# One 8 KB row per partition instead of two of 4 KB in the K and V loads of a decode kernel

## The chip, the cores and the metric

The kernel runs on one core of one Trainium2 chip. The metric is the time on the device in microseconds (us); below it is the median of several executions. A profile is a separate execution, recorded by the hardware profiler, and its span is a few us shorter than the timed runs.

## What is computed

Two identical layers of a decoder for one new token of each of B = 4 sequences. A layer is attention over a cache and then a gated FFN, each with a layernorm ahead and a residual add behind:

```python
def _A_ref(x, k_cache, v_cache, wq, wo):          # Hq = 32 heads, 8 K/V heads, Sk = 8192, Dh = 128
    q = (x @ wq).reshape(B, Sq, Hq, Dh) ...
    k = jnp.repeat(k_cache, rep, axis=1)           # rep = 4
    v = jnp.repeat(v_cache, rep, axis=1)
    scores = jnp.einsum("bhqd,bhkd->bhqk", q, k) * (Dh ** -0.5)
    p = _softmax(scores, axis=-1)
    o = jnp.einsum("bhqk,bhkd->bhqd", p, v)
    return o...reshape(B, Sq, Hq * Dh) @ wo
def _B_ref(x, w_gate, w_up, w_down):
    return (_silu(x @ w_gate) * (x @ w_up)) @ w_down

x = x + _A_ref(_layernorm(x), A_k_cache, A_v_cache, A_wq, A_wo)
x = x + _B_ref(_layernorm(x), B_w_gate, B_w_up, B_w_down)
# and both lines once more, with the same weights and caches
```

All is bfloat16. Each cache is 4 x 8 x 8192 x 128, 64 MB. Both layers read the same caches and weights. Softmax and the weighted sum over the cache don't depend on the order in which its rows are taken, as long as K and V take them in the same order.

## The kernel before

**Units.** The cache of one batch entry b and one K/V head g is cut into NCH = 4 chunks of CR = 2048 rows (512 KB). A unit is one such chunk, `("k", l, b, g, c)` or `("v", l, b, g, c)`, with l the layer. Two units make a pair, and a pair is what one DMA loads: 1 MB into one buffer, of which each unit uses one half. `KU` (line 251) pairs K units: heads g and g + 1 at the same chunk c. `VU` (line 254) pairs V units: chunks c and c + 1 of the same head.

**Buffers.** `ring` has NRING = 4 buffers of 1 MB, used in turn by K and V; `kept` has 5, in which five V pairs of every batch entry stay from layer 1 to layer 2. A buffer is given back (`release`, line 390) when the second unit of its pair has been issued to TensorE; `pump` (line 372) then issues the next load in the list on the SP queue, which waits for the semaphores of those that still read the buffer.

**A K unit** (`k_front`, line 409, and `k_back`, line 427). Rows of the cache lie on the partitions, 16 to a partition. TensorE transposes the 16 blocks of 128 x 128 into PSUM (line 417), in two halves of 8, each into one of three PSUM banks in turn; each half is copied to one of four `ktp` buffers by DVE or ACT (lines 246 and 248, five of eight to DVE). `k_back` multiplies them with the padded queries (line 433): four matmuls that accumulate all heads of one chunk in one score bank, bank 3 for even c and 4 for odd (`SBANK[c % 2]`). With the last head of a chunk comes `softmax_block` (line 443): a maximum on DVE (line 445) and an exponential with its sum on ACT (line 447). `k_back` of a unit is issued after `k_front` of the next one. After the last unit of the last chunk both are flushed, and `finalize` (line 452) starts the exchange of the maxima and the scaling and transposition of the probabilities, spread over the next units (`run_delayed`).

**A V unit** (`v_unit`, line 508): 32 matmuls with V blocks as weights and 4 probability columns (line 516), accumulated over the chunks of a head.

**Order.** The order of the pairs is written out by hand (lines 296 to 318), in phases: A1 (K of batch 0, layer 1), B1 (K of batch 1 mixed with V of batch 0), then for every b: C1 (V units around the FFN and the next query projection), A2 (K of layer 2 for b, mixed with V), B2 (V of layer 2, mixed with K of layer 1 for b + 2). `mix` (line 263) spreads the shorter list evenly over the longer; it sees pairs only, and there are 16 K pairs to a layer and batch entry. `A_of` (line 275) joins `KU(l, b, c)` for c = 0 to 3. Weight loads are put in at fixed places among the first 32 loads. [...]

Of the kernel before, what the change touches and what calls it, by code (L numbers as in the profile page):

```python
# [102 lines left out]
def bass_interleave_layers__gqa_block_cached__swiglu_ffn__decode_kernel(  # L103
# [13 lines left out]
    _, G, S, Dh = A_k_cache.shape  # L117
# [4 lines left out]
    P = 128  # L122
# [4 lines left out]
    CR = 2048  # L127
# [11 lines left out]
    with ExitStack() as es:  # L139
# [67 lines left out]
        T = _Sync(engines, prog)  # L207
# [41 lines left out]


        def KU(l, b, c):
            return [(("k", l, b, g, c), ("k", l, b, g + 1, c)) for g in range(0, G, 2)]

        def VU(l, b, g):
            return [(("v", l, b, g, c), ("v", l, b, g, c + 1)) for c in range(0, NCH, 2)]
# [7 lines left out]
        def mix(a, b):  # L263
# [9 lines left out]
            return r + b[k:]  # L273

        A_of = lambda l, b, cs: sum((KU(l, b, c) for c in cs), [])
        B_of = lambda l, b, gs: sum((VU(l, b, g) for g in gs), [])
        TAIL1 = [5, 5, 5]
# [60 lines left out]
        for pr in order:  # L338
            kind, l, b, g, c = pr[0]
            if kind == "v" and (g, c) in kept_ix:  # L340
                s = kept_ix[(g, c)]
                buf, key, sm = kept[:, s, :], f"kept{s}", sem_kept[s]
                fresh = l == 0
            else:
                s = nring % NRING
                nring += 1
                buf, key, sm = ring[:, s, :], f"ring{s}", sem_ring[s]
# [24 lines left out]
        def pump():  # L372
            while lptr[0] < len(loads):
                kind, x, sm = loads[lptr[0]]
                if kind == "w":
                    T.dma("sp", x[0], x[1], sm, writes=[x[2]])
                else:
                    pr, buf, key = x
                    if not released.get(key, True):
                        return  # L380
                    released[key] = False
                    kind, l, b, g, c = pr[0]
                    if kind == "k":
                        src = A_k_cache[b, g:g + 2, c * CR:(c + 1) * CR, :].rearrange("i (p t) d -> p i (t d)", p=P)
                    else:
                        src = A_v_cache[b, g, c * CR:(c + 2) * CR, :].rearrange("(i p t) d -> p i (t d)", i=2, p=P)
                    T.dma("sp", buf.rearrange("p (i x) -> p i x", i=2), src, sm, writes=[key])
                lptr[0] += 1

        def release(u):  # L390
# [269 lines left out]
        T.dma("sp", xrow[:], A_x.rearrange("b s d -> (b s) d"), sem_x, writes=["xrow"])  # L660
        T.dma("sp", wq_sb[:], A_wq.rearrange("(kt p) n -> p kt n", p=P), sem("sem_wq"), writes=["wq"])
        pump()
        xb = bank_bf(MISC)
        for nq in range(NQ):
# [10 lines left out]
        def do(u):  # L675
            if u[0] == "k":
                hv = k_front(u)
                if not hold["on"]:
                    flush()
                pending.append((u, hv))  # L680
                if u[3] == G - 1 and u[4] == NCH - 1:
                    flush()
            else:
                v_unit(u)
            run_delayed()
            pump()
# [118 lines left out]
```

## Time and profile before

| | |
|---|---|
| time, median of 3 (range) | 724.67 us (724.6 to 726.92) |
| span of the profile | 718.7 us |
| PE busy | 595.8 us (83%) |
| PE weight loads | 486.6 us (68%) |
| DVE busy | 299.5 us (42%) |
| ACT busy | 235.4 us (33%) |
| read from HBM | 261.36 MB, 364 GB/s over the span |
| K loads | 128 of 1 MB, median 8.0 us from issue to landing |
| V loads into the ring / kept | 88 / 20 of 1 MB, 8.3 / 13.0 us |
| transposes of K (line 417) | 4096, 303.4 us busy |
| score matmuls (line 433) | 1024, 113.8 us busy |
| V matmuls (line 516) | 4096, 128.1 us busy |

Busy time of TensorE overstates its load, since matmuls overlap. A load's time to landing includes the time that it stands behind earlier loads in the queue. "PE" is a matmul, "PEld" the load of its weights, "SPq" the queue that issues the DMAs. A line such as "PE ps L417 <- DMA ring<-in_A_k_cache_dram" says that TensorE's instructions of line 417 stood still for a K load to land; its numbers are the us in total, the times, and the longest.

### The profile page before, as it was taken

To read this page: it belongs to the slowest core of one execution; us is meant where nothing else is said; L and a number is where in the kernel's file an instruction comes from. 1 tells how busy PE (TensorE), PEld (TensorE's weight loads), DVE (VectorE), ACT (ScalarE), POOL (GpSimd) and SP (SyncE) were. 2 spreads that over 40 slices of the span, in tenths; PEclk is the share of its full clock that TensorE was granted. 3 is DMA by queue.
4 is the path that set the end of the run, shared out by engine and by line. 5 is a ranking of instruction groups with operands and counts; after the bars stand their busy time and mean duration, and the time that the engine had idled before them with its cause. 6 is when DMAs were issued, how large, how long until landed. Compare 5 with 4: busy or idle time off the path is not lost.

```text
span 718.7 us, 25091 instructions
## 1 busy us (share of the span) xinstructions
PE 595.8 (83%) x11552; PEld 486.6 (68%) x11552; DVE 299.5 (42%) x635; ACT 235.4 (33%) x296; POOL 0.7 (0%) x6
## 2 busy tenths in 40 slices
PE   3877878887989898897889989987898866999776
PEld 3755656667867676777766776766876666866565
DVE  2544533432445444442355525552255501355401
ACT  0444433320345334430344424530154400255200
POOL 0000000000000000000000000000000000000000
PEclk9999888975699788975799979995599855699755
DMA  8999999999699999999899999999899989599992
GB/s 350 388 388 407 397 399 375 403 401 386 235 374 398 363 353 399 352 411 393 294 391 399 384 403 382 385 409 402 314 386 383 393 339 408 181 370 389 370 402 80
DMA packets 71914, 262.99 MB, mean 366 GB/s; under 512 B 3960, under 2 KB 9856, under 8 KB 71296
## 3 DMA queue, kind: packets, MB, share of 16 engines
q1 hardware_dynamic: 71808, 261.38, 94.9%
q8 instruction: 90, 1.47, 0.8%
q14 instruction: 16, 0.13, 0.0%
HBM read 261.36 MB, written 0.00 MB: 364 GB/s over the span
## 4 chain that ended last, share of the span: by engine, by line
PE 46%; DMA 45%; DVE 3%; issue 3%; SPq 1%; ACT 1%; ACTq 0%
DMA ring<-in_A_k_cache_dram 29%; PE ps L417 24%; DMA ring<-in_A_v_cache_dram 14%; PE ps L516 6%; PE ps L433 6%; PE ps L581 2%; DMA wq_sb<-in_A_wq_dram 2%; PE ps L605 2%; SPq L92 1%; PE ps L557 1%; PE ps L641 1%; PE ps L540 1%; PE ps L488 1%; DVE negm L445 1%; ACT ktp L248 1%
## 5 line engine op out<-in xcount | busy, mean ns | idle before, releaser
L417 PE MATMUL ps<-ident,ring 128*128 128x128 bf16 x4096 | 303.4, 233 | 42.3 <-DMA ring<-in_A_k_cache_dram 42.0
L417 PEld LDWEIGHTS ps<-ident,ring 128*128 128x128 bf16 x4096 | 258.9, 105 | 94.7 <-DMA ring<-in_A_k_cache_dram 52.7
L246 DVE COPY ktp<-ps 128x1024 bf16<-128x1024 bf16 x320 | 215.7, 689 | 205.3 <-PE ps L417 204.0
L248 ACT ACTIVATE ktp<-ps 128x1024 bf16<-128x1024 bf16 x192 | 195.9, 1023 | 267.4 <-PE ps L417 267.4
L433 PE MATMUL ps<-ktp,qpad 128*32 128x512 bf16 x1024 | 113.8, 414 | 3.5 <-ACT ktp L248 3.0
L516 PE MATMUL ps<-pp,ring 128*128 128x4 bf16 x2816 | 88.6, 166 | 27.1 <-DMA ring<-in_A_v_cache_dram 13.5
L516 PEld LDWEIGHTS ps<-pp,ring 128*128 128x128 bf16 x2816 | 82.9, 101 | 37.6 <-issue 19.3
L433 PEld LDWEIGHTS ps<-ktp,qpad 128*32 128x32 bf16 x1024 | 27.6, 93 | 37.9 <-ACT ktp L248 6.4
L573 ACT ACTIVATE lnv<-var,eps_sb 128x4 f32<-128x4 f32 x10 | 3.0, 298 | 145.6 <-DVE var L560 145.6
L524 DVE TENSOR_TENSOR oT<-ps,invL 128x4 bf16<-128x4 f32 x64 | 10.7, 167 | 93.7 <-PE ps L516 93.3
L516 PE MATMUL ps<-pp,kept 128*128 128x4 bf16 x1280 | 39.5, 166 | 8.9 <-DMA kept<-in_A_v_cache_dram 6.2
L516 PEld LDWEIGHTS ps<-pp,kept 128*128 128x128 bf16 x1280 | 37.6, 103 | 11.7 <-issue 6.1
L447 ACT ACTIVATE pp<-ps,negm 128x512 bf16<-128x512 f32 x32 | 22.0, 687 | 31.2 <-DVE negm L445 29.7
L581 PE MATMUL ps<-xnT,wq_sb 128*128 128x4 bf16 x640 | 18.7, 166 | 10.9 <-DMA wq_sb<-in_A_wq_dram 7.8
L445 DVE TENSOR_REDUCE negm<-ps 128x1 f32<-128x512 f32 x32 | 22.1, 690 | 11.7 <-PE ps L433 10.3
L581 PEld LDWEIGHTS ps<-xnT,wq_sb 128*128 128x128 bf16 x640 | 18.1, 104 | 11.4 <-DMA wq_sb<-in_A_wq_dram 7.9
L540 PE MATMUL ps<-oT,wo_sb 128*128 128x4 bf16 x640 | 21.9, 166 | 3.6 <-DVE oT L524 2.6
L540 PEld LDWEIGHTS ps<-oT,wo_sb 128*128 128x128 bf16 x640 | 19.4, 102 | 7.1 <-issue 3.6
L488 PE MATMUL ps<-ident,pp 128*128 128x128 bf16 x128 | 15.0, 311 | 1.0 <-DVE pp L478 1.0
L488 PEld LDWEIGHTS ps<-ident,pp 128*128 128x128 bf16 x128 | 13.0, 145 | 1.1 <-DVE pp L478 1.1
L248 ACT ACTIVATE pp<-ps 128x1024 bf16<-128x1024 bf16 x6 | 6.1, 1024 | 21.9 <-PE ps L488 21.9
L641 PE MATMUL ps<-hT,wd_sb 128*128 128x4 bf16 x280 | 8.5, 166 | 5.0 <-issue 3.8
(66 smaller groups left out, 151.9 us busy)
## 6 DMA issues: line engine op xcount, KB each, us to landing
ring<-in_A_k_cache_dram SPq DMA_DIRECT2D x128, 1024.0 KB, 8.0
ring<-in_A_v_cache_dram SPq DMA_DIRECT2D x88, 1024.0 KB, 8.3
kept<-in_A_v_cache_dram SPq DMA_DIRECT2D x20, 1024.0 KB, 13.0
wq_sb<-in_A_wq_dram SPq DMA_DIRECT2D x1, 4096.0 KB, 12.4
wo_sb<-in_A_wo_dram SPq DMA_DIRECT2D x4, 1024.0 KB, 13.7
wg_sb<-in_B_w_gate_dram SPq DMA_DIRECT2D x2, 896.0 KB, 13.5
wu_sb<-in_B_w_up_dram SPq DMA_DIRECT2D x2, 896.0 KB, 13.8
wd_sb<-in_B_w_down_dram SPq DMA_DIRECT2D x2, 896.0 KB, 11.3
```

The costliest lines, as they stand in the source:

```text
L246: T.op("dve", lambda e: e.tensor_copy(dst, src), reads=reads, writes=writes)
L248: T.op("act", lambda e: e.activation(dst, src, ACTF.Copy), reads=reads, writes=writes)
L417: T.op("pe", lambda e: e.matmul(stg[:, t * P:(t + 1) * P], lhsT=ap[:, blk * Dh:(blk + 1) * Dh], rhs=ident[:], is_transpose=True, start=Tru ...
L433: T.op("pe", lambda e: e.matmul(ps[32 * j:32 * (j + 1), bk * BW:(bk + 1) * BW], lhsT=qp, rhs=ktp[:, s, (j % 2) * 512:(j % 2 + 1) * 512], s ...
L445: T.op("dve", lambda e: e.tensor_reduce(negm[:, q, c:c + 1], bank(bk), AX.X, ALU.max, negate=True), reads=[f"pb{bk}"], writes=[f"negm{q}_{ ...
L447: T.op("act", lambda e: e.activation(pp[:, q, c * 512:(c + 1) * 512], bank(bk), ACTF.Exp, bias=negm[:, q, c:c + 1], scale=1.0, accum_out=l ...
L488: T.op("pe", lambda e: e.matmul(stg[:, t * P:(t + 1) * P], lhsT=pp[:, q, blk * P:(blk + 1) * P], rhs=ident[:], is_transpose=True, start=Tr ...
L516: T.op("pe", lambda e: e.matmul(ps[:, bk * BW:bk * BW + REP], lhsT=ap[:, (NM * j + m) * Dh:(NM * j + m + 1) * Dh], rhs=pp[:, q, col:col + ...
L540: T.op("pe", lambda e: e.matmul(ps[:, OPJ * BW + nq * B:OPJ * BW + (nq + 1) * B], lhsT=wo_sb[:, h, nq * P:(nq + 1) * P], rhs=oT[:, l, h, : ...
L581: T.op("pe", lambda e: e.matmul(misc[:, h * B:(h + 1) * B], lhsT=wq_sb[:, kt, h * Dh:(h + 1) * Dh], rhs=xnT[:, kt * B:(kt + 1) * B], start ...
L605: T.op("pe", lambda e: e.matmul(ps[:, bk * BW + fo * B:bk * BW + (fo + 1) * B], lhsT=w_sb[:, kt, fo * P:(fo + 1) * P], rhs=xnT[:, kt * B:( ...
L641: T.op("pe", lambda e: e.matmul(misc[:, nq * B:(nq + 1) * B], lhsT=wd_sb[:, fo, nq * P:(nq + 1) * P], rhs=hT[:, fo * B:(fo + 1) * B], star ...
```

## The change

A K pair becomes two chunks of one head, as a V pair has been. Both chunks then lie together in the cache, 4096 rows, and each partition takes 32 rows that follow each other: 8 KB in one run, where a K load had 4 KB from each of two heads and a V load 4 KB from each of two chunks. The first unit of a pair takes the first 16 of the 32 rows of each partition, the second the other 16, in K and V alike. It is meant to let every DMA descriptor move twice as much, with half as many of them.

With it the order of the K units changes: it was all eight heads of chunk 0, then of chunk 1, and so on; it becomes chunks 0 and 1 of head 0, of head 1, to head 7, and then chunks 2 and 3. Score banks 3 and 4 fill side by side, and both chunks' softmax blocks come with head 7. Number, size and place of the loads, and all other code, stay.

```diff
         def KU(l, b, c):
-            return [(("k", l, b, g, c), ("k", l, b, g + 1, c)) for g in range(0, G, 2)]
+            return [(("k", l, b, g, c), ("k", l, b, g, c + 1)) for g in range(G)] if c % 2 == 0 else []
...
                     kind, l, b, g, c = pr[0]
-                    if kind == "k":
-                        src = A_k_cache[b, g:g + 2, c * CR:(c + 1) * CR, :].rearrange("i (p t) d -> p i (t d)", p=P)
-                    else:
-                        src = A_v_cache[b, g, c * CR:(c + 2) * CR, :].rearrange("(i p t) d -> p i (t d)", i=2, p=P)
-                    T.dma("sp", buf.rearrange("p (i x) -> p i x", i=2), src, sm, writes=[key])
+                    cache = A_k_cache if kind == "k" else A_v_cache
+                    src = cache[b, g, c * CR:(c + 2) * CR, :].rearrange("(p t) d -> p (t d)", p=P)
+                    T.dma("sp", buf, src, sm, writes=[key])
```

## The prediction

> **What bounds the kernel now.** I read the page top down, then the waits, then the transfers, then stretches of the timeline. First the page: the slices with the DMA engines' share, and the queue that carries the loads.
>
> ```profile
> PEclk9999888975699788975799979995599855699755
> DMA  8999999999699999999899999999899989599992
> GB/s 350 388 388 407 397 399 375 403 401 386 235 374 398 363 353 399 352 411 393 294 391 399 384 403 382 385 409 402 314 386 383 393 339 408 181 370 389 370 402 80
> q1 hardware_dynamic: 71808, 261.38, 94.9%
> ```
>
> The DMA engines are busy nearly always; the weak slices (235, 294, 314, 181 GB/s) are the four FFN passes between the layers (phase C1), and the last is the final FFN. So the loads are the first suspect. But the chain of waits says that TensorE is as much on the path:
>
> ```profile
> PE 46%; DMA 45%; DVE 3%; issue 3%; SPq 1%; ACT 1%; ACTq 0%
> ```
>
> and the waits tell how much TensorE would gain from faster loads:
>
> ```profile
> PEld ps L417 <- DMA ring<-in_A_k_cache_dram: 52.7, 60, 3.1
> PE ps L417 <- DMA ring<-in_A_k_cache_dram: 42.0, 38, 2.8
> PE ps L516 <- DMA ring<-in_A_v_cache_dram: 13.5, 13, 1.6
> PE ps L516 <- DMA kept<-in_A_v_cache_dram: 6.2, 7, 1.6
> ```
>
> TensorE waits 42.0 + 13.5 + 6.2 = 61.7 us for K and V, in pieces of 0.3 to 2.8 us. That is the most that any speed-up of these loads could bring without speeding up TensorE. The windows by stage separate the two limits (columns: length, busy us of PE, PEld, DVE, ACT and POOL, granted clock, DMA share, GB/s):
>
> ```profile
> 13.10:160.00 146.90, 120.52 (x1896) 93.00 (x1896) 66.64 (x117) 56.45 (x67) 0.00 (x0) 0.89 1.03 395
> 167.70:211.00 43.30, 37.86 (x820) 32.51 (x820) 17.27 (x43) 12.27 (x17) 0.00 (x0) 0.73 0.86 312
> 211.00:321.00 110.00, 98.80 (x1705) 78.10 (x1706) 53.40 (x98) 45.65 (x55) 0.00 (x0) 0.86 1.00 380
> 364.00:485.00 121.00, 105.23 (x1922) 83.49 (x1920) 58.38 (x107) 48.52 (x60) 0.00 (x0) 0.90 1.02 396
> ```
>
> 167.7 to 211 is an FFN pass and the K work piled up behind it: no TensorE wait for a load stands there, TensorE is the limit, the ring fills and the DMA share falls to 0.86. Its like are 327 to 364, 490.5 to 528.5 and 601 to 644 (in all 43.3 + 36.8 + 38 + 43 = 161 us). In the others (13 to 160, 211 to 321, 364 to 485, 528.5 to 596, 644 to 706) the loads are the limit most of the time.
>
> Now the price of a load by its row length. The trace has both kinds: wq comes in 8 KB rows, K and V in 4 KB rows. DMA queries of 4 to 12.5 us (wq alone) and 100 to 110 us (K and V alone, queue full):
>
> ```profile
> DMA packets 444, 3.64 MB, mean 428 GB/s; under 512 B 0, under 2 KB 0, under 8 KB 0
> ...
> DMA packets 1059, 4.09 MB, mean 409 GB/s; under 512 B 63, under 2 KB 63, under 8 KB 1058
> ```
>
> The packet records behind them agree: median 159 ns for the 60,416 packets of 4 KB, 309 ns for the 512 of 8 KB; so two of 4 KB cost 318, one of 8 KB 309, about 9 ns saved. (The 1 KB rows of wo, 48 ns, and the 3.5 KB rows of wg and wu, 144 ns, lie on the same line: some 9 ns fixed and 37 ns per KB.)
>
> **What the Trainium skill says.** "DMA: Bandwidth & Descriptors", section Why small descriptors are slow (HBM only): each packet has a fixed overhead in the engine, and each DMA operation carries descriptor metadata. The trace agrees in kind, with 9 ns of 159. The same page, Where 436 GB/s comes from, puts the ceiling of the SBUF ports at 435 GB/s: 428 for the 8 KB rows lies near it, so no row length brings more than about 6% over 409. Its Latency and other measured facts warns that copies slow down when the rows of neighbouring partitions lie 512 KiB or more apart; here they lie 4 KB apart before and 8 KB after, as in wq, so I expect no such loss. "TensorE: Matmul & The Clock Gate", section HAM oscillation, says that TensorE's waits for loads can drop its clock. The trace agrees: after the 2.80 us wait at 44 to 47 us, the second block of 16 transposes took 1.89 us instead of 1.07.
>
> **The change, part by part.**
>
> *Rows.* A 1 MB load is 16 packets of 4 KB per DMA engine now and becomes 8 of 8 KB. From the packet records: 16 x 159 + 9 (the semaphore packet) = 2.553 us, which is the spacing seen between landings while the queue is full (2.53 to 2.57 us). After: 8 x 309 + 9 = 2.481 us, 0.072 us less (2.8%); by the two windows 1 - 409/428 = 4.4%, but the wq window holds only 444 packets. I take 3.1%, 0.08 us. All 108 + 128 = 236 loads change: 236 x 0.08 = 19 us of queue time. It counts only where the loads set the pace. From the windows, time at full-queue speed is length x rate/409: 146.9 x 395/409 = 142; 110 x 380/409 = 102; 121 x 396/409 = 117; 67.5 x 379/409 = 63 and 62 x 378/409 = 57 for the last two stages; together 481, less 24 for the weights (9.4 MB, whose rows stay) = 457 us. 457 x 3.1% = 14.2 us.
>
> Not all of it is kept. A K unit costs TensorE 1.07 + 0.40 us of overlapping busy time and starts 1.33 us after the last, so a K load feeds 2.66 us of TensorE, more than 2.48; a V load feeds about 2.1 (32 matmuls take 1.03). In runs of K alone TensorE is just the limit already; mixed with V it has air, and the 61.7 us of waits for K and V are several times 14. In the stretches with few waits (2.8 us of K waits in 515 to 565) part is lost. I take 80%: 11.4 us; the bounds are 60% (8.5) and 100% with 4.4% (20).
>
> *Order of K units.* Same number and size of loads, same places in the order, same releases, since a pair of units stays one load. What moves is the softmax: per pass over K it stood after units 8, 16, 24, 32 and now after 15 and 16, then 31 and 32. Each is one reduction (DVE, 0.69 us) and one exponential (ACT, 0.69 + 0.19). The timeline of before shows one in a stretch with TensorE at full pace:
>
> ```profile
> 199.12 1.05 PE L417 MATMUL ps<-ident,ring 128*128 128x128 bf16 x16
> ...
> 200.44 1.07 PE L417 MATMUL ps<-ident,ring 128*128 128x128 bf16 x16
> 200.56 0.69 DVE L445 TENSOR_REDUCE negm<-ps 128x1 f32<-128x512 f32 x1
> ...
> 201.34 0.69 ACT L447 ACTIVATE pp<-ps,negm 128x512 bf16<-128x512 f32 x1
> ...
> 201.76 1.07 PE L417 MATMUL ps<-ident,ring 128*128 128x128 bf16 x16
> ```
>
> TensorE's 1.33 us beat (199.12, 200.44, 201.76) is not broken: a single softmax costs nothing, hidden beside transposes. Two on consecutive units press harder: two units have 4 evictions of about 0.86 us on average (0.689 on DVE five times in eight, 1.023 on ACT three), 3.3 us of engine time, plus 2 x 1.57 = 3.1 for the softmaxes, 6.4 in all against 2 x 2.66 = 5.3 that the two engines have. Behind them stand the evictions of the next transposes, and TensorE waits for these when its three banks are full: (6.4 - 5.3)/2 = 0.55 us at worst per pair, and 0 if the three banks and four ktp buffers absorb it. There are 8 such pairs inside a pass: 0 to 4.4 us, most of it in stretches where loads are waited for anyway. I take 0.5.
>
> *New wait.* The first K unit of the next two chunks adds to the score bank that the pair's first exponential still reads. The old run gave 8 units for that, the new one two: about 2.66 us. From the start of the chunk's last score matmuls (200.10) to the end of its exponential (its sum is read at 201.93, 0.19 us) it took 2.02 us: it just fits, cost 0; if it doesn't, TensorE waits some 0.3 us, 8 times, with the transposes of the next unit queued behind.
>
> *End of a pass.* Both last softmaxes now come in one flush; the reduction of the last chunk, on which the max exchange hangs, waits for that of the chunk before: 0 to 0.7 us, 8 times. The score matmuls between them waited for evictions anyway (0.20 and 0.38 us at 75.86 and 242.12), so I take 0.2 x 8 = 1.6 at most, half of it on the path: 0.8.
>
> Sum: -11.4 + 0.5 + 0.8 = about -10.1; 724.67 - 10.1 = 714.6.
>
> **The rivals.** *All of it arrives and more*: the windows' 4.4% holds, and fewer waits keep the clock up. 457 x 4.4% = 20 us: 704.6. For it: the clock of 0.5 to 0.7 after waits. Against: K runs need 2.66 us of TensorE per load. *Nothing moves*: TensorE's own 46% of the chain stretches to fill what the loads give up, or the rows of wq were quick only because the compute engines were idle: 724. Against: in 100 to 110 us all engines work and the packets still take 159. *Slower*: rows bring nothing in the mixed stages, and pairs of softmaxes cost 0.55 + 0.3 for each of 8 and 0.7 for each of 8 ends, 12.4 us with half of it again for a halved clock after each stop (the slow blocks at 48.70): 724.67 + 10 = about 735. Against: a single softmax shows no stop at all, and ring slack is four loads deep.
>
> **How the numbers follow.** Forecast (708 to 720): 0.60. All and more (below 708): 0.15. No change: 0.09. Slower: 0.16. The range takes 703 to 724: it holds the forecast, nearly all of the first rival and the second, and leaves out the slower one and a tail. Faster by over 0.3% (below 722.5): 0.75, within: 0.09, slower: 0.16.
>
> **What would show it.** Right: 8 KB packets near 309 ns; full-queue stretches at 420 GB/s or more; K waits of TensorE down by some 10 us in the load-bound windows; DMA idle before the FFN passes up; the FFN windows unchanged in length. Wrong on rows: the rate stays near 409. Wrong on order: new TensorE waits for ACT at L433, or longer waits for the DVE's gm. It fails as a whole if TensorE's busy time grows by what its waits lose.

## The result, and the profile after

The changed kernel takes 718.71 us (median of 3, 716.16 to 718.84) against 724.67: a ratio of 0.9897, interval 0.9853 to 0.9941. Measured once more beside the experiments below it took 717.79 us against 724.56, ratio 0.9884 (0.982 to 0.9948). So it gains 7.5 to 8.4 us, with 3 to 5 us of doubt to either side; the forecast was a gain of 10.1. Some executions of several kernels ran slower, most of them at a lower granted clock: the medians below count all executions, the ratios and the gains worked out from them only the others, so that a gain can differ by a us or two from the difference of two medians.

The page of the kernel after, the slices with clock, DMA share and rate, and the load queue:

```profile
PEclk9998798885699889975699969995599955599755
DMA  8999999999599999999799999999999989599992
GB/s 355 395 395 416 374 404 380 407 401 379 202 402 407 388 370 391 366 414 368 248 409 389 387 382 372 366 423 420 330 370 417 394 320 422 209 374 419 387 389 82
q1 hardware_dynamic: 41600, 261.38, 92.7%
```

The same bytes travel in 41,600 packets instead of 71,808, and their share of the DMA engines' time falls from 94.9% to 92.7% although the span is shorter. The best slices reach 416 to 423 GB/s (411 before). Two of the weak slices are weaker here (202 and 248 where 235 and 294 stood), but a second profile of the same kernel shows 233 and 280, so that is no effect of the change; several slices in between stay at 366 to 374. The chain of waits:

```profile
PE 54%; DMA 37%; DVE 4%; issue 4%; ACT 1%; SPq 0%
```

DMA's share of the chain falls from 45% to 37%, TensorE's rises from 46% to 54%. This can't be put down to the rows: with the order alone and rows of 4 KB (below) the shares are 37% and 53%. TensorE's waits for loads:

```profile
PEld ps L415 <- DMA ring<-in_A_k_cache_dram: 45.1, 49, 3.0
PE ps L415 <- DMA ring<-in_A_k_cache_dram: 35.7, 32, 2.7
PE ps L514 <- DMA ring<-in_A_v_cache_dram: 19.0, 16, 2.7
PE ps L514 <- DMA kept<-in_A_v_cache_dram: 5.1, 6, 1.6
```

The waits for K lose 6.3 us (42.0 to 35.7), those for V gain 5.5 (13.5 to 19.0); their sum hardly falls, 61.7 to 59.8 (61.0 in the second profile, with 39.8 for K). What falls more is TensorE's busy time, here from 595.8 to

```profile
PE 590.9 (83%) x11552; PEld 485.0 (68%) x11552; DVE 300.1 (42%) x635; ACT 236.4 (33%) x296; POOL 0.7 (0%) x6
```

The packet records give a median of 309 ns for the 8 KB packets. The semaphore records give the time between one load's last landing and the next one's: at the queue's own pace it falls from 2.55 to 2.48 us, as forecast.

### The profile page after: what moved, and what is told of

It is laid out like the page before. It is cut to its first block, busy times and chain, and to the rows that moved or that the text cites. A ratio compares the mean times of both kernels' runs of the same rounds, so it can differ in the third digit from the quotient of the medians.

```text
span 714.4 us, 25097 instructions
## 1 busy us (share of the span) xinstructions
PE 590.9 (83%) x11552; PEld 485.0 (68%) x11552; DVE 300.1 (42%) x635; ACT 236.4 (33%) x296; POOL 0.7 (0%) x6
## 3 DMA queue, kind: packets, MB, share of 16 engines
q1 hardware_dynamic: 41600, 261.38, 92.7%
q8 instruction: 90, 1.47, 0.8%
## 4 chain that ended last, share of the span: by engine, by line
PE 54%; DMA 37%; DVE 4%; issue 4%; ACT 1%; SPq 0%
PE ps L415 28%; DMA ring<-in_A_k_cache_dram 25%; DMA ring<-in_A_v_cache_dram 10%; PE ps L514 9%; PE ps L431 7%; PE ps L579 3%; PE ps L603 2%; DMA wq_sb<-in_A_wq_dram 2%; PE ps L538 1%; PE ps L555 1%; PE ps L486 1%; PE ps L639 1%; DVE negm L443 1%; ACT ktp L248 1%; DVE rowm L462 1%
## 5 line engine op out<-in xcount | busy, mean ns | idle before, releaser
L415 PE MATMUL ps<-ident,ring 128*128 128x128 bf16 x4096 | 302.5, 233 | 36.1 <-DMA ring<-in_A_k_cache_dram 35.7
L431 PE MATMUL ps<-ktp,qpad 128*32 128x512 bf16 x1024 | 110.7, 407 | 3.2 <-ACT ktp L248 2.7
L579 PE MATMUL ps<-xnT,wq_sb 128*128 128x4 bf16 x640 | 18.8, 166 | 11.4 <-DMA wq_sb<-in_A_wq_dram 7.8
L246 DVE COPY pp<-ps 128x1024 bf16<-128x1024 bf16 x10 | 6.9, 692 | 11.0 <-PE ps L486 11.0
## 6 DMA issues: line engine op xcount, KB each, us to landing
wq_sb<-in_A_wq_dram SPq DMA_DIRECT2D x1, 4096.0 KB, 12.4
```

Of the source, the lines that this page charges most:

```text
L246: T.op("dve", lambda e: e.tensor_copy(dst, src), reads=reads, writes=writes)
L415: T.op("pe", lambda e: e.matmul(stg[:, t * P:(t + 1) * P], lhsT=ap[:, blk * Dh:(blk + 1) * Dh], rhs=ident[:], is_transpose=True, start=Tru ...
L431: T.op("pe", lambda e: e.matmul(ps[32 * j:32 * (j + 1), bk * BW:(bk + 1) * BW], lhsT=qp, rhs=ktp[:, s, (j % 2) * 512:(j % 2 + 1) * 512], s ...
L579: T.op("pe", lambda e: e.matmul(misc[:, h * B:(h + 1) * B], lhsT=wq_sb[:, kt, h * Dh:(h + 1) * Dh], rhs=xnT[:, kt * B:(kt + 1) * B], start ...
```

## The experiments

They ran in three groups on three chips, each group beside the kernel before on the same chip. A ratio is against that one, and runs of different groups are compared by their ratios.

**Rows and order apart.** My theory (A) was that the rows bring nearly all and the order costs about 1 us; the rivals, that rows bring 11 and the order eats 5 (B), or that the gain comes from the order (C). The changed kernel again, as the measure:

> The changed kernel once more, beside the kernel before on the same chip, as the measure for the three others. Theory A (rows bring about 7 us, the new order of K units costs about 1): ratio 0.990 to 0.993, about 718.5 us. Theory B (rows bring the forecast 11, the order of K units eats 5): the same 718.5. Theory C (the order brings it, rows nothing): the same.

Measured: 717.79 us, ratio 0.9884 (0.982 to 0.9948).

The order alone, rows of 4 KB:

```diff
-                    src = cache[b, g, c * CR:(c + 2) * CR, :].rearrange("(p t) d -> p (t d)", p=P)
-                    T.dma("sp", buf, src, sm, writes=[key])
+                    src = cache[b, g, c * CR:(c + 2) * CR, :].rearrange("(i p t) d -> p i (t d)", i=2, p=P)
+                    T.dma("sp", buf.rearrange("p (i x) -> p i x", i=2), src, sm, writes=[key])
```

> The new order of K units alone: a pair is two chunks of one head, but each partition still takes two rows of 4 KB. Theory A: 725.5 us, +1 (0 to +2). Theory B: about 730, +5. Theory C (the gain comes from the order): about 719. All expect packets of 4 KB at a median of 159 ns and landings 2.55 us apart while the queue is full.

Measured: 724.06 us, ratio 0.9967 (0.9937 to 0.9997): 2.4 us less than before, 0.2 to 4.6. The order costs nothing; if anything it gains. From this run to the changed kernel, both in the new order, the rows bring 6.0 us (0.9 to 11.1).

The rows alone, in the old order:

```diff
-            return [(("k", l, b, g, c), ("k", l, b, g, c + 1)) for g in range(G)] if c % 2 == 0 else []
+            return [(("k", l, b, g, c), ("k", l, b, g + 1, c)) for g in range(0, G, 2)]
...
+                    c -= c % 2
                     src = cache[b, g, c * CR:(c + 2) * CR, :].rearrange("(p t) d -> p (t d)", p=P)
```

> 8 KB rows alone: loads of 1 MB in one run per partition, but K units in the old order, so a K pair takes the 4096 rows of one head for its two heads and the scores are those of other rows than the names say (work of every engine unchanged). Theory A: 717.5 us, -7. Theory B: 713, -11.5. Theory C: 724.5. Packets of 309 ns in all.

Measured: 716.0 us, ratio 0.9858 (0.9798 to 0.9918): 10.3 us less, 5.9 to 14.6. (The pairs of chunks c and c + 1 load the same rows here, so half of the K cache is read twice and half not at all; packets at 309 ns and a pace of 2.48 us show no effect of that.) C falls: the gain is mainly the rows'. B falls on the order's side, which is no loss of 5. Whether the two parts add up (10.3 + 2.4 against 8.4 for both) lies within the intervals and isn't settled.

**The price of the order where TensorE sets the time.** Both orders with half of every K and V load left out (512 KB, of which both units of a pair take the same half):

```diff
-                home[u] = (buf[:, i * NB * Dh:(i + 1) * NB * Dh], key, i == 1)
+                home[u] = (buf[:, 0:NB * Dh], key, i == 1)
...
-                    src = cache[b, g, c * CR:(c + 2) * CR, :].rearrange("(p t) d -> p (t d)", p=P)
-                    T.dma("sp", buf, src, sm, writes=[key])
+                    src = cache[b, g, c * CR:(c + 1) * CR, :].rearrange("(p t) d -> p (t d)", p=P)
+                    T.dma("sp", buf[:, 0:NB * Dh], src, sm, writes=[key])
```

New order:

> The changed kernel with half of every K and V load left out: 512 KB, of which both units of a pair take the same half, so the second units work on the wrong rows. Loads can no longer be the limit, so this shows what TensorE and its helpers need alone. If the 61.7 us of waits for K and V are really air, 724.7 - 62 = about 660 us, less what the clock gains. If TensorE's own pace is the limit close behind (which would explain that faster loads bring only 6 of 11 us), about 700.

Old order:

> The kernel before (old order of K units) with half of every K and V load left out, both units of a pair working on the same half: TensorE alone sets the time, so that beside the same cut of the changed kernel (620.83 us) the price of the order itself stands bare. Forecast: the new order costs 0.5 + 0.8 us, up to 6 with every bound at its worst: 615 to 619.5 here. If the new order is cheaper, because the first softmax of a pass comes later: 623 or more.

Measured: 620.83 us, ratio 0.8586 (0.853 to 0.8642), in the new order and 625.42 us, ratio 0.8664 (0.8617 to 0.8712), in the old one. The new order is the quicker one by 5.6 us, with a doubt of about 5.3 (worked out from the two intervals): a gain at the edge of what can be told, and no sign of the loss that was forecast. The larger finding is the level. The page of the new order with half loads:

```profile
PE 567.2 (91%) x11552; PEld 469.6 (75%) x11552; DVE 299.2 (48%) x635; ACT 235.9 (38%) x296; POOL 0.7 (0%) x6
...
q1 hardware_dynamic: 41600, 137.65, 66.5%
```

I had read the 61.7 us of waits as the most that faster loads could bring. Half loads bring 97 us (717.79 to 620.83). Between the profiles of the two it is 92 us: TensorE's idle time falls by 67.6 us, of which 56.6 are waits for K and V (61.0 to 4.4), and its busy time by 24.6 (591.8 to 567.2) while the granted clock rises from 0.800 to 0.833 on average. Busy time times clock is the same in both, 473 us (591.8 x 0.800 and 567.2 x 0.833). So the bound held as far as it was meant, without a faster TensorE; what it left out is that TensorE itself gets faster.

**What a load's queue time is worth.** Here all loads are made, but much of the work on them is left out: 8 of a K unit's 16 transposes, and 12 of the 16 V matmuls of a chunk.

```diff
-            for hf in range(2):
+            for hf in range(1):
...
-            return halves
+            return halves * 2
...
-            for m in range(NM):
+            for m in range(1):
...
```

With 8 KB rows:

> The changed kernel with most of TensorE's work on K and V left out: of a K unit only the first 8 of 16 transposes and one of the two evictions (the scores take that half twice), of a V unit 4 of the 16 matmuls of a chunk (the rest of the weighted sum is missing). All loads stay. Loads should then set nearly the whole time: 236 loads x 2.481 + 34 us for the weights + start and end (about 15 + 12) = 646 us, plus a few us for each FFN pass: about 655. What tells the theories apart is its distance to the same cut of the kernel before: 236 x 0.072 = 17 us if each row pair saves 9 ns (the packet records), 26 us if the two windows' 4.4% were right, 10 or less if landings are set by something other than the packets.

With 4 KB rows and the old order:

> The kernel before with the same work left out as in the light cut of the changed kernel. 17 us longer than that one (about 672) if the saving is 9 ns per pair of rows; 26 if 4.4%; 10 or less if something other than packets sets the landings.

Measured: 669.16 us (ratio 0.9266, 0.9215 to 0.9317) and 679.08 us (0.9426, 0.9372 to 0.948): 9.9 us apart (by the ratios 11.6, with a doubt of 5.4), though TensorE has less to do. Both are above the forecasts of 655 and 672. The distance falls at "10 or less", which was to mean that something other than the packets sets the landings; the doubt still reaches up to 17. The pair also differs in the order of the K units. DMA queries of 100 to 130 us, 8 KB rows first, then 4 KB:

```profile
DMA packets 1711, 12.46 MB, mean 415 GB/s; under 512 B 192, under 2 KB 192, under 8 KB 192
```

```profile
DMA packets 3168, 12.24 MB, mean 408 GB/s; under 512 B 187, under 2 KB 187, under 8 KB 3165
```

And the dose the other way, four rows of 2 KB, in the new order:

```diff
-                    src = cache[b, g, c * CR:(c + 2) * CR, :].rearrange("(p t) d -> p (t d)", p=P)
-                    T.dma("sp", buf, src, sm, writes=[key])
+                    src = cache[b, g, c * CR:(c + 2) * CR, :].rearrange("(i p t) d -> p i (t d)", i=4, p=P)
+                    T.dma("sp", buf.rearrange("p (i x) -> p i x", i=4), src, sm, writes=[key])
```

> The changed kernel (new order) with four rows of 2 KB per partition in each K and V load instead of one of 8 KB: the dose the other way. By the line through the known packets (9 ns fixed and 37 ns per KB) a packet takes 83 ns and a load 32 x 83 + 9 = 2.665 us, 0.184 more than with 8 KB rows: 43 us of queue time over 236 loads. If queue time turns into time at the rate seen between 8 KB and 4 KB rows in this order (724.06 - 717.79 = 6.3 us of 17), +16 us, 734; if nearly all of it does, +35 or more, 753.

Measured: 741.61 us, ratio 1.0249 (1.018 to 1.0317), between the two forecasts (734 and 753). The queue in its page, and a query of 100 to 110 us:

```profile
q1 hardware_dynamic: 132224, 261.38, 96.5%
```

```profile
DMA packets 1933, 3.86 MB, mean 386 GB/s; under 512 B 56, under 2 KB 57, under 8 KB 1932
```

The packets take a median of 86 ns (83 were worked out), and loads land 2.70 us apart (2.665). So a load is slower with more packets from 2 to 8 KB rows, 2.70, 2.55, 2.48 us, near what a fixed cost per packet gives.

All these landings side by side. From the semaphore records of each profile: the spacing of last landings at the queue's pace, how many of the 246 come at it (less than 0.1 us later) or earlier, how many come later, and by how much in all. The last column takes of these later ones those whose load had been issued more than 2.5 us before the load ahead of it landed. The shortest way from issue to landing in these profiles is 4.7 to 5.1 us, about 2.5 of them the load's own turn, so such a load was issued in time, and TensorE did not hold it back.

| kernel | pace, us | at pace or earlier | later | sum of the excess, us | of it, issued in time, us |
|---|---|---|---|---|---|
| 2 KB rows, new order | 2.70 | 187 | 59 | 57.5 | 31.1 (47) |
| before (4 KB) | 2.55 | 171 | 75 | 67.5 | 43.0 (64) |
| 4 KB rows, new order | 2.55 | 174 | 72 | 71.5 | 43.8 (59) |
| after (8 KB), first profile | 2.48 | 166 | 80 | 79.4 | 44.4 (61) |
| after, second profile | 2.48 | 163 | 83 | 81.6 | 45.6 (66) |
| 8 KB rows, old order | 2.48 | 158 | 88 | 76.0 | 43.9 (69) |
| light work, 4 KB | 2.56 | 214 | 32 | 26.0 | 17.1 (28) |
| light work, 8 KB | 2.48 | 204 | 42 | 33.4 | 22.6 (36) |

The quicker the pace, the more landings miss it, and the more they lose. From before to after 246 x 0.07 = 17 us are taken off the pace and 12 (first profile) come back as later landings; the sum of the spacings falls by 4.4 us, as the span does (718.7 to 714.4). From 2 KB to 8 KB rows the pace times 236 gives 52 us and the time falls by (1.0249 - 0.9884) x 724 = 26, with a doubt of 7. With light work it is 10 to 12 of 19, and the doubt there is 5. Rows of 8 KB for 4 KB bring 10.3 of 17 us in the old order and 6.0 in the new. So a third to 60% of the queue time becomes time.

**Why not all: depth, or lags of single DMA engines.** Two theories. (I) A fetch of instructions takes one DMA engine for about 1 us (90 fetches, "q8 instruction: 90, 1.47 MB" in the page), and a load lands with its slowest engine. (II) With four buffers TensorE gives them back too late to keep the queue full. More fetches, by semaphore waits on the idle GpSimd:

```diff
+        for _ in range(23040):
+            nc.gpsimd.wait_ge(prog["pool"], 2)
```

> The changed kernel with 11,520 semaphore waits that are long fulfilled on GpSimd, which otherwise has nothing to do: 0.74 MB of instructions more, about 45 fetches of 16 KB beside the 90 that TensorE's program needs. Theory I (a fetch sits on one DMA engine for 0.6 us or more and every load lands with its slowest engine, so that fetches cause the slow landings of loads that stand in the queue: 47 us of excess for 90 fetches): 135 fetches, excess about 70 us, time up by 8 to 20 us, to 726 to 738. Theory II (these landings are late because TensorE gives buffers back late): 717 to 719, no change.

Measured: 1028.17 us (ratio 1.413), and it doesn't decide. The kernel has 11,520 wait instructions, one for each two waits of the source, each took about 89 ns, and so GpSimd itself set the end at 1026 us. The result was sent at

```profile
720.55 0.29 SPq L775 DMA_DIRECT2D out_dram<-xrow  x1
```

against 712.84 and 714.86 in the two profiles of the changed kernel. The added fetches went through another queue (q14, 106 packets in the page instead of 16, and 0.87 MB instead of 0.13), and only 62 of the 90 added packets fell in the first 720 us. A delay of 6 to 8 us in one profile is within what the kernel varies by, and so is a sum of excess of 87 us against 79.4 and 81.6: (I) is neither shown nor ruled out.

Ring depth. Three buffers:

```diff
-    NRING = 4
+    NRING = 3
```

> The changed kernel with three ring buffers of 1 MB instead of four. Theory II (late release by TensorE limits what faster loads bring): the queue runs dry far more often, 740 to 760 us. Theory I: depth matters less, 720 to 730.

Four kept V pairs instead of five, with a ring of four, and then of five (NRING = 5 beside it):

```diff
-    NRET = 5
+    NRET = 4
```

> The changed kernel with four kept V pairs instead of five and the ring of four, the measure for the deeper ring: 4 loads of 2.48 us more. If queue time turns into time at the rate seen so far (40 to 60%), +4 to +6 us, 722 to 724; if all of it does, +10, 728.

> The changed kernel with five ring buffers and four kept V pairs instead of four and five, so 4 loads of 1 MB more are made (10 us of queue time). Theory II: the deeper queue gives back more than these cost: against the same with four ring buffers and four kept pairs 8 to 15 us less. Theory I: 0 to 5 us less.

Measured: 799.14 us with three (ratio 1.0972, 1.0883 to 1.1061); 725.08 with four and four kept (1.0005, 0.9976 to 1.0034); 696.48 with five and four kept (0.9576, 0.9527 to 0.9625). TensorE's waits, three buffers and then five:

```profile
PE ps L415 <- DMA ring<-in_A_k_cache_dram: 70.8, 52, 3.7
PE ps L514 <- DMA ring<-in_A_v_cache_dram: 42.6, 32, 3.9
```

```profile
PE ps L415 <- DMA ring<-in_A_k_cache_dram: 27.0, 21, 2.7
PE ps L514 <- DMA ring<-in_A_v_cache_dram: 10.4, 11, 2.9
```

and the rate by slices with five:

```profile
GB/s 354 394 395 416 407 408 412 416 419 418 217 379 423 416 379 422 410 421 415 273 402 421 420 409 416 420 420 417 349 383 421 418 394 420 224 389 414 395 385 51
```

Between the FFN passes most slices now run at 400 to 423 GB/s. Against the same kept pairs with a ring of four, the fifth buffer takes 28.6 us off, though the loads and rows are the same; later landings fall from 83 (76.8 us) to 58 (51.3 us). So depth has a large effect, as (II) says, and a larger one than (II) forecast: 28.6 us where 8 to 15 were expected, and 799 us with three buffers where 740 to 760 were. The four loads more were a miss too: 725.08 is 7 to 9 us over the changed kernel, with a doubt of 5, where +4 to +6 was forecast; their queue time is 9.9, so most of it became time.

But (II) isn't the whole account. By the table, more than half of the excess, 43.0 of 67.5 us before and 44.4 of 79.4 after, stands at loads that were issued in time, and TensorE can't have delayed these; whether fetches did is open. What grows from 4 KB to 8 KB rows with all the work is the rest: the part issued in time stays at 43 to 46 us, the other rises from 24.5 to 35.0 (36.0 in the second profile), as (II) has it. From 2 KB to 8 KB rows both parts grow, by 13 and 9 us, and in the light pair 5.5 of the 7.4 us more stand at loads issued in time. With the fifth buffer both parts fall (42.5 to 27.6 and 34.3 to 23.6), so a deeper queue helps with either. Late release fits what comes back from 4 KB to 8 KB rows with full work, by these few profiles; it isn't shown as the cause of the rest.

The version with five ring buffers and four kept pairs and 8 KB rows is faster than both kernels, at the same work. Whether the rows bring more with five buffers, which would test (II) directly, was not tried.

## Why the prediction was right

The total is right because the price of a row was measured well; the rest has some luck in it. The rows brought somewhat less than the 11.4 us forecast (10.3 and 6.0, see below), the order gained where a small loss was forecast, and the share of 80% was a guess.

**The price of a row.** The packet records gave 309 against 159 ns, and the pace went from 2.55 to 2.48 us, the 2.553 and 2.481 that were worked out. The 4.4% of the two windows was too much: the light cuts differ by 415 to 408 GB/s, 1.7%, over a window that includes some late landings, and the pace by 2.8%. The wq window was too short to price a row. No loss by the 8 KB step between partitions was seen, so the Trainium skill's warning on row pitch ("DMA: Bandwidth & Descriptors", Latency and other measured facts) did not bear on this case, as argued. (Its figures are for copies within HBM and hardly fall at the 512 KiB that the prediction names, 207 GB/s against 214 at full rate; the large loss is at 2 MiB and above. No run here shows either.)

**How much of it becomes time.** The term "457 us at full-queue speed x 3.1% x 80% = 11.4 us" measured 10.3 us in the old order (5.9 to 14.6) and 6.0 in the new (0.9 to 11.1). In shares, 457 of the 236 x 2.553 = 603 us of queue time, and 80% of that, is 61%, at the upper end of the third to 60% that was measured. The reason given for the 80% is not what the runs point to, though. I took the loads' stages as bound by loads and took something off for runs of K in which TensorE is just the limit. But with half loads TensorE needs 621 us, and with light work the loads need 669; neither of them sets the 718. The two are tied by the buffers between them, as the ring of five shows, and a quicker pace is partly given back as later landings.

One reading behind the 80% was wrong as well. A V unit is 16 matmuls, not 32 (4096 in 256 units), and a whole V load feeds TensorE for 0.8 us, not 2.1. In the timeline of before, one V load's 32 matmuls stand between the transposes of two K units, the second of them at 199.12:

```profile
198.31 0.95 PE L516 MATMUL ps<-pp,ring 128*128 128x4 bf16 x32
```

A K load and a V load together take TensorE 2.66 + 0.8 = about 3.5 us (without the output projection), against 5.1 us in the queue. So mixed stretches have more air than the prediction thought. Two slips don't bear on the result: four evictions of 0.81 us, not 0.86, give the 3.3 us; and 12.4 us "with half of it again" is 18.6, not the 10 that was added for the slower rival.

**"The most that any speed-up could bring."** The 61.7 us of waits bound the gain only for a TensorE that keeps its speed: half loads bring 97. The prediction cited "TensorE: Matmul & The Clock Gate", section HAM oscillation, for waits that lower the clock, but did not carry it into the bound. (The page speaks of idle times beyond some 3.4 us; the prediction's slow block followed a wait of 2.80.) Over the runs with all of TensorE's work, busy time times mean clock stays within 469 to 477 us, while the clock goes from 0.768 (three buffers, 120 us of waits for K and V) over 0.799 (before, 61.7) to 0.833 (half loads, 4.4). The three profiles with 8 KB rows in full loads have a TensorE busy time of 589.7 to 591.8 us, the two with 4 KB rows 595.8 and 600.1, and part of the gain stands there. That the shorter waits cause the higher clock is argued, not shown: with five buffers the waits fall to 40 us, and the clock stays at 0.803.

**The order of the units.** Forecast +1.3 us; measured -2.4 (0.2 to 4.6 less), so the direction was wrong, and that made up for part of what the rows fell short. The worry was two softmax blocks on consecutive units. The timeline of after, in the first pass over K, transposes and the two reductions:

```profile
45.76 0.68 DVE L443 TENSOR_REDUCE negm<-ps 128x1 f32<-128x512 f32 x1
...
47.70 1.07 PE L415 MATMUL ps<-ident,ring 128*128 128x128 bf16 x16
47.82 0.69 DVE L443 TENSOR_REDUCE negm<-ps 128x1 f32<-128x512 f32 x1
...
49.03 1.07 PE L415 MATMUL ps<-ident,ring 128*128 128x128 bf16 x16
...
50.68 1.01 PE L415 MATMUL ps<-ident,ring 128*128 128x128 bf16 x15
```

One beat of 1.33 us becomes 1.65 (49.03 to 50.68): 0.3 us at this pair, between the bounds 0 and 0.55. At the end of the pass the reduction of the last chunk does come behind the other one's, but the exchange of maxima starts no later after the last transposes. After, then before:

```profile
74.17 1.07 PE L415 MATMUL ps<-ident,ring 128*128 128x128 bf16 x16
76.03 1.28 DVE L443 TENSOR_REDUCE negm<-ps 128x1 f32<-128x512 f32 x2
...
77.56 0.27 PE L459 MATMUL ps<-identf,gm 128*1 128x128 f32 x1 [0.99 <-DVE gm L452]
```

```profile
73.86 1.07 PE L417 MATMUL ps<-ident,ring 128*128 128x128 bf16 x16
...
77.23 0.27 PE L461 MATMUL ps<-identf,gm 128*1 128x128 f32 x1 [0.98 <-DVE gm L454]
```

77.56 - 74.17 = 3.39 us, 77.23 - 73.86 = 3.37: this one end costs 0.02, not the 0.2 taken. Why the new order should be quicker isn't explained; that the first softmax of a pass comes later, out of the stretch behind an FFN pass, was not tested by itself.

**Signs named beforehand.** Packets of 309 ns: seen. Full-queue stretches at 420 GB/s: seen in single slices (422, 423). More DMA idle time around the FFN passes: not seen, since the 202 and 248 GB/s of the first profile are 233 and 280 in the second. K waits down by some 10 us: 6.3 and 2.2 in the two profiles, and the V waits took most of it back. New waits of TensorE at the score matmuls: none of weight (for ktp on ACT 3.0 us before, 2.7 after).

## What to carry to other kernels

Price a longer row from the packet records of rows that the kernel already moves, and multiply by the number of packets per DMA engine. Then expect less than that: where loads and compute take turns through a few buffers, part of a quicker pace can return as later landings, here 40 to 65% of it. If TensorE needs 621 us with half the loads, the loads 669 with less work on them, and the kernel 718, look at the buffers first: one more ring buffer brought 28.6 us where doubling the row brought about 8.

## What was not expected of the hardware

Two packets of half the length cost only 9 to 13 ns more than one (2 KB 86 ns, 4 KB 159, 8 KB 309), yet 2 KB rows cost 26 us more than 8 KB rows in the same order (1.0249 against 0.9884 of the time before). An instruction with fulfilled semaphore waits took about 89 ns on GpSimd (11,520 in 1026 us). A ring of three instead of four buffers of 1 MB cost about 79 us (1.0972 against 0.9884).
